# Retention and SwiGLU in one kernel: the output-weight sums of two quads per GpSimd instruction, the order of the second tile's first sums, and the place of tile 0's results

## The chip, the core and the metric

The kernel runs on one core of a Trainium2 chip. The metric is device time in microseconds (us), the median of several executions. A profile is one further execution, recorded by the hardware profiler; its span runs from the first to the last recorded instruction. The engines are named as in the profile: PE (matmul), DVE (vector), ACT (scalar), POOL (GpSimd) and SP, which here only issues transfers. "ACTq" and "SPq" are the transfers that ACT and SP issue.

## The reference

Retention for 8 batches and 8 heads, then a SwiGLU block over the 4608 tokens that come out of it. All of it is float32.

```
scores = scale * q @ k.T                       # per batch and head, 576 x 576, head size 64
ret = scores * D                               # D[i, j] = gamma_h ** (i - j) for i >= j, else 0
attn = ret @ v
x = attn.transpose(0, 2, 1, 3).reshape(4608, 512)
g, val = x @ w_gate, x @ w_val                 # 512 x 1536 each
out = (g / (1 + exp(-g)) * val) @ w_out        # 1536 x 512
```

## The kernel before

**Tiles.** The tokens are cut into tile 0 (512 tokens) and tiles 1 to 4 (1024 tokens each). A "tick" (`tick`) does the retention of one pair of heads: PE forms scores, states and values in the tiles `inner` and `outer`, and ACT, DVE and SP prepare the operands of the next pair. A pair needs its transposed keys (`kT`, L492), its scaled keys (`kn`, L507) and the masked scores (`ret`, L580). Ticks 10 to 13 stand between the down products of tile 0.

**Tile 0** is computed plainly: `up0` makes the twelve blocks `hid0[0]` to `hid0[11]` of the hidden activation, and `down0` (L864) multiplies them with the output weights in the order of `down_order`, four matmuls of 512 columns for each block, into the banks A, B, C and E. `out0` (L869, L870) then copies the four banks with ACT to `part[4:8]` and stores them.

**Tiles 1 to 4** use a fast matrix multiplication after Strassen and Winograd on two levels. The weights lie in three "quads" (`qd` 0 to 2). The up product of a quad goes through seven sets of operands, `SETS = (1, 2, 6, 7, 4, 5, 3)`. Outer sums make sets 5, 6, 7, 4 of the weights (`w_outer`) and 5, 6, 3, 7 of the tokens (`x_outer`); inner sums (`w_inner`, `x_inner`) make four further blocks of a set. A set in `PLAIN` goes without inner sums. In tile 1 and quad 0 these are sets 1, 4, 5 and 3, so that only sets 2, 6 and 7 need inner sums there. One step of the up product, called a slot here, is two matmuls (L1183) into one bank; a plain set has 8 slots, another has 7. The result of a slot is added from the bank by DVE (L1040) or copied by ACT (L1215); finished blocks go through silu on ACT (L1197) and a product on DVE or POOL (L1198) into `hid`.

**Sums of the weights.** In tile 1 POOL makes the sums of the up weights as it goes, and SP stores each set to memory (`store`, L1116 to L1119) for tiles 2 to 4, which load them. The sums of the output weights are made once, while tile 0 is computed (`out_sums`, L886): a list of events, `OUT_SUMS`, is gone through for each quad, and each of its 26 operands is stored with one transfer (L954, `dn<-rest`). POOL does quads 0 and 1, DVE quad 2. Two of the operands are needed negated for POOL, which ACT does (`negate`, L916). POOL's results go to 256-column places in `rest`, six at first and ten later; DVE's go to 22 places. A place is used again when its store has landed. The lists are emitted in groups of three operands, one group of DVE and one of POOL after each block of `down0`; POOL's first ten groups stand earlier, after blocks 10 and 11 of `up0`.

**Order.** All engines run a recorded program in order. The order of each engine's instructions, SP's transfers included, is the order in which the Python code issues them. At the end of tile 0 (`m >= 9`) `early_sums` puts the first sums of tile 1 behind POOL's sums of the output weights: `w_outer(5)`, `w_inner(1)` and its store, `w_outer(7)`, `w_inner(2)` and its store. The rest of quad 0's sums stand at slots of tile 1 in `up_stage` (`later(at, ...)`): x sums of set 2 at 0, of 6 at 10, of 7 at 18, of 1 at 28; weights of 6 (outer at 4, inner at 6), 7 (inner at 14), 4 (outer at 22, inner at 24), 5 at 32 and 3 at 37; set 1 of the next quad at 42. The two retention pairs that follow are loaded by SP behind slots 13 and 30.

**Places.** `part` lies in `rest` from `dn_at` on. `w_dn` of quad 0 is `part[0:4]`, and of quad 1 `part[4:8]`, so that these parts can be written only when POOL has read the output weights there and SP has stored those of them that are operands themselves. `hid` of quad 0 lies over `hid0[0]` to `hid0[7]`. Sets 6, 5 and 4 of the quad-0 weights are written over `hid0[1]` and `[3]`, `[4]` and `[6]`, `[5]` and `[7]`; each must wait until `down0` has read these.

Of the kernel before, what the change touches and what calls it, by code (L numbers as in the profile page):

```python
# [131 lines left out]
def kernel(  # L132
# [32 lines left out]
    nc = tc.nc  # L165
# [691 lines left out]
            nc.vector.tensor_tensor(out=hid0[f], in0=pair[1], in1=s, op=ALU.mult)  # L857


    down_order = [8, 9, 10, 4, 5, 11, 6, 7, 0, 1, 2, 3]  # L860

    def down0(f):
        for i, bank in enumerate(banks):
# [1 line left out]
                             start=(f == down_order[0]), stop=(f == down_order[-1]))  # L865

    def out0():
        for i, (bank, o) in enumerate(zip(banks, part[4:8], strict=True)):
            nc.scalar.copy(out=o, in_=bank)  # L869
            nc.sync.dma_start(out=out[i * P : (i + 1) * P, :], in_=o)  # L870

# [18 lines left out]

    pool_places = [rest[:, sum_at + TB * i : sum_at + TB * (i + 1)] for i in range(6)]
    more_places = [rest[:, raw_at + TB * i : raw_at + TB * (i + 1)] for i in range(16) if i % 4]
    x0_places = [rest[:, x0_at + TB * i : x0_at + TB * (i + 1)] for i in range(8)]
    vector_places = x0_places + more_places[6:] + [rest[:, part_at + TB * i : part_at + TB * (i + 1)] for i in range(8)]

    def events_of(text):
        r = []
# [12 lines left out]
    negatives = [x_odd[:, r, 640 : 640 + TB] for r in (2, 3)] + more_places[4:6]  # L912

    def negate(qd):
        for n, s in enumerate((3, 5)):
            nc.scalar.mul(out=negatives[2 * qd + n], in_=w_dn[:, qd, s // 2, s % 2], mul=-1.0)  # L916

    def out_sums(qd):
# [8 lines left out]
        eng, sum_places = (nc.vector, vector_places) if qd + 1 == NQ else (nc.gpsimd, pool_places)  # L927
        events = events_of(OUT_SUMS if qd + 1 == NQ else signed)

        def view(s):  # L930
            if s > 13:
                return negatives[2 * qd + s - 14]
            return w_dn[:, qd, s // 2, s % 2] if s < 8 else place[s]

        def used(e):
            return [e[1]] if e[0] is None else [int(a) for a in e[1][2:]]

        def release(k):

            for s in list(place):  # L940
                for e in events[k + 1 :]:
                    if s in used(e):
                        break
                    if s == e[0]:
                        free(place.pop(s))
                        break
                else:
                    free(place.pop(s))

        def do(k):  # L950
            e = events[k]
            if e[0] is None:
                _, slot, i = e
                nc.sync.dma_start(out=dn_ops[i][:, qd * TB : (qd + 1) * TB], in_=view(slot))  # L954
            else:
                new = sum_places.pop(0)
                add(eng, e[1], view, new)
                if e[0] in place:
                    free(place[e[0]])
                place[e[0]] = new  # L960
            release(k)

        r, ends = [], [k for k, e in enumerate(events) if e[0] is None]
        for g in range(0, N, 3):
            lo, hi = ends[g - 1] + 1 if g else 0, ends[min(g + 2, N - 1)] + 1

            def group(lo=lo, hi=hi):
                for k in range(lo, hi):
                    do(k)

            r.append(group)
        return r
# [121 lines left out]
    def w_sets(qd):  # L1094

        up = lambda n, k: w_up[:, qd, :, 2 * n : 2 * n + 2, k, :]
        sets = {1: up(0, 0), 2: up(0, 1), 7: up(1, 0), 3: up(1, 1), 5: hid[:, qd, 2:4, 0:2], 6: hid[:, qd, 0:2, 2:4], 4: hid[:, qd, 2:4, 2:4]}
        blocks = (extra_at(0, 1024), extra_at(1536, 1024), rest[:, x0_at + 1024 : x0_at + 2048])
        new = {o: blocks[(qd + i) % 3].rearrange("p (g j x) -> p g j x", g=2, j=4) for i, o in enumerate(SETS)}
# [12 lines left out]

        def store(o, new_ones):
            dst = up_sets[qd][SETS.index(o)]
            if new_ones:
                return [lambda: nc.sync.dma_start(out=dst[:, 6 * P :], in_=new[o].rearrange("p g j x -> p (g j x)"))]  # L1116
            raw = dst[:, 0 : 6 * P].rearrange("p (g x) -> p g x", g=2)
            return [lambda: nc.sync.dma_start(out=raw[:, :, P:], in_=sets[o][:, :, 0]),
                    lambda: nc.sync.dma_start(out=raw[:, :, 0:P], in_=sets[o][:, :, 1, P:])]  # L1119

        return sets, new, outer_sums, inner_sums, store

    def early_sums():

        x_outer = x_sets(1)[0]
        _, _, w_outer, w_inner, store = w_sets(0)
        p = [w_outer(5), w_inner(1) + store(1, True), w_outer(7), w_inner(2) + store(2, True)]
        v = [f for o in (5, 6, 3, 7) for f in x_outer(o, nc.vector)]
        return p, v

    def up_stage(n):
# [18 lines left out]
        def later(at, *fs):  # L1150
            after.setdefault(at, []).extend(fs)
# [288 lines left out]
        if t + AHEAD < NP:  # L1440
            load(t + AHEAD)

    groups = [(qd, group) for qd in range(NQ - 1) for group in out_sums(qd)]
    last_groups = out_sums(NQ - 1)
    todo = [m for m in range(3, len(order))]
    plan = []

# [8 lines left out]
    for f in range(2, NF):  # L1456
        round_until({4: 12, 6: 13, 8: 14, 9: 15, 10: 16, 11: 17}.get(f, f + 2))
        plan.append(lambda f=f: up0(f, range(HP)))
        if f - 1 in tick_at and f < 7:
            plan.append(lambda t=tick_at[f - 1]: next_load(t))  # L1460
        if f in tick_at and f > 2:
            plan.append(lambda t=tick_at[f]: tick(t, HP, FIRST))
            if tick_at[f] == HP + 1:
                plan.append(end_transposes)
        if f in (7, 10, 11):
            plan.append(lambda t=tick_at[f]: next_load(t))
        for _ in range({10: 7, 11: 3}.get(f, 0)):
            if f >= (7, 10, NF)[groups[0][0]]:
                if f + 1 == NF and more_places:
                    plan.append(lambda places=more_places[:4]: pool_places.extend(places))  # L1470
                    more_places.clear()
                if len(groups) % 9 == 0:
                    plan.append(lambda qd=groups[0][0]: negate(qd))
                plan.append(lambda group=groups.pop(0)[1]: group())
    assert not todo and len(groups) < 9
    for f in plan:
        f()
    tick_at = {1: 10, 3: 11, 6: 12, 8: 13}
    for m, f in enumerate(down_order):
# [5 lines left out]
        if last_groups:  # L1485
            last_groups.pop(0)()
        if groups:
            groups.pop(0)[1]()
# [12 lines left out]
    out0()  # L1501
    done = FIRST
# [59 lines left out]
```

## Time and profile before

| what | value |
| --- | --- |
| median of 3 runs | 1025.83 us (1025.13 to 1030.31) |
| the profiled execution | 1026.62 us, of which the span is 1024.9 us |
| DVE busy | 713.3 us (70%) |
| ACT busy | 286.3 us (28%) |
| POOL busy | 557.5 us (54%) |
| granted TensorE clock | full in all 40 slices |
| transfers | 194.38 MB, mean 190 GB/s |

Tile 0's up and down products end at about 176 us, tile 1's up product runs from there to about 329 us with ticks in its second half, and the down product of tile 1 follows. In the timeline view each line gives the start, the length, the engine, the line of the code, the operands and how many instructions were merged into it; in brackets stands how long the engine had been idle before it and what ended this. "x8" matmuls of L1183 are two slots, "x4" is one.

### The profile page before, as it was taken

How to read it: one execution, taken by the hardware profiler on the slowest of the kernel's cores; microseconds unless marked ns; L12 is line 12 of the kernel's file. 1: busy time of each engine (PE TensorE's matmuls, PEld its weight loads, DVE VectorE, ACT ScalarE, POOL GpSimd, SP SyncE). 2: the span in 40 equal slices, each digit the busy share in tenths (PEclk: the TensorE clock that was granted, in tenths of full speed). 3: DMA queues.
4: the chain of work that ended last, by engine and by line, in shares of the span. 5: the costliest groups of instructions: out<-in, count | busy, mean ns of one | idle time of the engine just before them, and what ended most of it. 6: DMA issues, size and time to landing. Idle time of an engine off the chain costs nothing.

```text
span 1024.9 us, 21387 instructions
## 1 busy us (share of the span) xinstructions
PE 1003.7 (98%) x8336; PEld 823.0 (80%) x8336; DVE 713.3 (70%) x1215; ACT 286.3 (28%) x638; POOL 557.5 (54%) x602
## 2 busy tenths in 40 slices
PE   6999989899999999999999999999999999999998
PEld 5654545788888888888888888888888888888887
DVE  5488877588787766876778688848585767566644
ACT  4465531122332411132332111133320012232110
POOL 3400178997563208665656247755582486566515
PEclk9999999999999999999999999999999999999999
DMA  9999877966496897656658767444455454445552
GB/s 244 253 272 239 202 203 247 275 202 176 120 266 157 221 238 225 194 157 174 187 181 225 195 186 210 148 141 144 157 193 155 144 185 154 143 147 188 175 161 100
DMA packets 281612, 194.38 MB, mean 190 GB/s; under 512 B 212968, under 2 KB 251112, under 8 KB 281512
## 3 DMA queue, kind: packets, MB, share of 16 engines
q1 hardware_dynamic: 247112, 93.52, 35.6%
q10 hardware_dynamic: 33760, 99.10, 29.5%
q8 instruction: 66, 1.08, 0.4%
q0 software_dynamic: 640, 0.39, 0.2%
q14 instruction: 34, 0.28, 0.1%
HBM read 154.04 MB, written 38.93 MB: 188 GB/s over the span
## 4 chain that ended last, share of the span: by engine, by line
PE 69%; DVE 2%; issue 1%; SPq 0%; DMA 0%; DVEq 0%; ACT 0%
PE bankC L1183 9%; PE bankB L1183 9%; PE bankA L1183 9%; PE bankE L1183 9%; PE bankB L1378 7%; PE bankE L1378 7%; PE bankC L1378 7%; PE bankA L1378 6%; PE outer L1183 2%; PE inner L1183 2%; DVE rest L1040 2%; PE outer L532 1%; PE outer L559 1%; PE inner L573 1%; PE inner L543 1%
## 5 line engine op out<-in xcount | busy, mean ns | idle before, releaser
L1040 POOL TENSOR_TENSOR rest<-rest 128x512 f32<-128x512 f32 (+1 forms) x141 | 150.3, 1077 | 156.1 <-DVE rest L1040 114.1
L1198 POOL TENSOR_TENSOR arena<-rest,io 128x256 f32<-128x256 f32 x156 | 113.8, 740 | 88.6 <-ACT io L1197 83.2
L1197 ACT ACTIVATE io<-rest 128x256 f32<-128x256 f32 x192 | 79.4, 417 | 212.0 <-DVE rest L1040 149.6
L1183 PE MATMUL bankB<-rest,arena 128*128 128x256 f32 x448 | 114.9, 381 | 1.0 <-DVE rest L1040 0.9
L1040 DVE TENSOR_TENSOR rest<-bankB,rest 128x512 f32<-128x512 f32 x116 | 78.5, 685 | 47.7 <-PE bankB L1183 32.2
L1183 PE MATMUL bankA<-rest,arena 128*128 128x256 f32 x412 | 105.4, 381 | 1.4 <-POOL rest L1040 0.9
L1183 PE MATMUL bankC<-rest,arena 128*128 128x256 f32 x416 | 106.4, 380 | 0.4 <-DVE rest L1040 0.2
L1040 DVE TENSOR_TENSOR rest<-bankA,rest 128x512 f32<-128x512 f32 x110 | 74.5, 684 | 45.9 <-PE bankA L1183 21.3
L1040 DVE TENSOR_TENSOR rest<-bankC,rest 128x512 f32<-128x512 f32 x110 | 74.7, 685 | 32.0 <-PE bankC L1183 18.9
L1183 PEld LDWEIGHTS bankB<-rest,arena 128*128 128x128 f32 x448 | 84.5, 190 | 13.8 <-POOL rest L1040 1.2
L1183 PE MATMUL bankE<-rest,arena 128*128 128x256 f32 x372 | 95.0, 380 | 0.4 <-DVE rest L1040 0.3
L1040 DVE TENSOR_TENSOR rest<-bankE,rest 128x512 f32<-128x512 f32 x106 | 71.8, 685 | 31.3 <-PE bankE L1183 14.8
L1183 PEld LDWEIGHTS bankA<-rest,arena 128*128 128x128 f32 x412 | 77.7, 190 | 13.6 <-DVE rest L1040 1.8
L1183 PEld LDWEIGHTS bankC<-rest,arena 128*128 128x128 f32 x416 | 78.3, 190 | 12.6 <-DVE rest L1040 1.4
L1040 POOL TENSOR_TENSOR arena<-arena 128x256 f32<-128x256 f32 (+1 forms) x80 | 74.4, 953 | 12.1 <-DMA up<-arena 6.2
L1183 PEld LDWEIGHTS bankE<-rest,arena 128*128 128x128 f32 x372 | 69.9, 190 | 11.7 <-DVE rest L1040 1.6
L886 POOL TENSOR_TENSOR rest<-rest 128x256 f32<-128x256 f32 x43 | 33.4, 800 | 53.8 <-DVE rest L407 36.6
L1378 PE MATMUL bankB<-arena 128*128 128x256 f32 x264 | 61.0, 381 | 0.0
L1378 PE MATMUL bankE<-arena 128*128 128x256 f32 x264 | 60.8, 380 | 0.0
L1378 PEld LDWEIGHTS bankE<-arena 128*128 128x128 f32 x264 | 49.9, 190 | 6.9
L1378 PEld LDWEIGHTS bankB<-arena 128*128 128x128 f32 x264 | 49.8, 190 | 6.9
L886 POOL TENSOR_TENSOR arena<-arena 128x768 f32<-128x768 f32 x24 | 47.0, 1961 | 15.3 <-DVE arena L1198 14.7
(267 smaller groups left out, 1881.1 us busy)
## 6 DMA issues: line engine op xcount, KB each, us to landing
arena<-up ACTq DMA_DIRECT2D x63, 896.0 KB, 4.6
arena<-dn ACTq DMA_DIRECT2D x65, 384.0 KB, 3.5
arena<-dn SPq DMA_DIRECT2D x39, 384.0 KB, 3.2
dn<-rest SPq DMA_DIRECT2D x78, 128.0 KB, 2.0
out_dram<-rest SPq DMA_DIRECT2D x35, 256.0 KB, 3.1
qk<-in_q_dram SPq DMA_DIRECT2D x108, 72.0 KB, 3.1
qk<-in_k_dram SPq DMA_DIRECT2D x108, 72.0 KB, 3.1
up<-arena SPq DMA_DIRECT2D x14, 512.0 KB, 2.9
```

The costliest lines, as they stand in the source:

```text
L532: m = nc.tensor.matmul(value(i, hl, c), s["v"][rows, at], ret[rows, c % 2 if whole(i) else hl, c // 2], start=start, stop=start, skip_grou ...
L543: nc.tensor.matmul(z[half[hl], r, c], s["kn"][chunk(i, hl, 2 * c + r)], s["v"][rows, at], start=True, stop=True, skip_group_check=True)
L559: nc.tensor.matmul(xr[half[hl]] if c + 1 == NC else value(i, hl, c), state[half[hl], c, :], s["qT"][half[hl], ts(c, L)], start=False, stop ...
L573: nc.tensor.matmul(sc[chunk(i, hl, 2 * c + r)[0], r if whole(i) else hl, c], kT[half[hl], at], qT[half[hl], at], start=True, stop=True, sk ...
L886: eng.tensor_tensor(out=dst, in0=srcs[0], in1=srcs[1], op=ALU.add if op[0] == "add" else ALU.subtract)
L1040: eng.tensor_tensor(out=out, in0=a, in1=b, op=ALU.add if sign > 0 else ALU.subtract)
L1183: m = nc.tensor.matmul(b[:, g * TB : (g + 1) * TB], w[:, g], x, start=(opens and g == 0), stop=True, skip_group_check=True)
L1197: nc.scalar.activation(out=s, in_=src[:, 0:TB], func=AF.Silu)
L1198: (nc.vector if busy and o != 2 else nc.gpsimd).tensor_tensor(out=hid[:, qd, 2 * H + h, 2 * T + t], in0=src[:, TB : 2 * TB], in1=s, op=ALU ...
L1378: nc.tensor.matmul(b[:, m * TB : (m + 1) * TB], lhs[:, qd, ts(m, P)], w[:, qd], start=(opens and qd == 0 and m == 0), stop=(qd == NQ - 1), ...
```

## The change

The sums of the output weights of quads 0 and 1 are made together: each POOL instruction of L886 works on 512 columns (256 of either quad) and each store of these carries both quads. POOL has seven places of 512 columns, all from the start; DVE's places go from 22 to 18. All nine groups of POOL now stand after blocks of `down0`, and both negations stand together behind `up0`, of 512 columns each. `down_order` reads the blocks that sets 6, 5 and 4 overwrite earlier and blocks 0 and 2 last; `out0` copies to these two and to `io`. The early sums are those of sets 2, 5 and 6, of weights and tokens. Set 1 of the weights of quad 0 is summed and stored at slot 28 of tile 1, and the blocks that hold inner sums take turns in another order in quad 0.

```
-    down_order = [8, 9, 10, 4, 5, 11, 6, 7, 0, 1, 2, 3]
+    down_order = [8, 9, 1, 3, 10, 4, 6, 11, 5, 7, 0, 2]
...
-        for i, (bank, o) in enumerate(zip(banks, part[4:8], strict=True)):
+        for i, (bank, o) in enumerate(zip(banks, (hid0[0], hid0[2], io[:, 0:512], io[:, 512:1024]), strict=True)):
             nc.scalar.copy(out=o, in_=bank)
             nc.sync.dma_start(out=out[i * P : (i + 1) * P, :], in_=o)
...
+    both = lambda lo, step: rest[:, lo : lo + 2 * step].rearrange("p (q x) -> p q x", q=2)[:, :, 0:TB]
+    pool_places = [both(sum_at + 2 * TB * i, TB) for i in range(3)]
+    wide_places = [both(raw_at + TB * i, TB * step) for i, step in ((1, 1), (3, 2), (9, 1), (13, 1))]
+    vector_places = x0_places + [rest[:, raw_at + TB * i : raw_at + TB * (i + 1)] for i in (11, 15)] + [rest[:, part_at + TB * i : part_at + TB * (i + 1)] for i in range(8)]
...
-    def negate(qd):
+    negatives = [x_odd[:, 2:4, 640 : 640 + TB], both(raw_at + 6 * TB, TB)]
+    def negate():
         for n, s in enumerate((3, 5)):
-            nc.scalar.mul(out=negatives[2 * qd + n], in_=w_dn[:, qd, s // 2, s % 2], mul=-1.0)
+            nc.scalar.mul(out=negatives[n], in_=w_dn[:, 0:2, s // 2, s % 2], mul=-1.0)
...
-                nc.sync.dma_start(out=dn_ops[i][:, qd * TB : (qd + 1) * TB], in_=view(slot))
+                nc.sync.dma_start(out=dn_ops[i].rearrange("p (q x) -> p q x", q=NQ)[:, qs], in_=view(slot))
...
+        turns = [(qd + i) % 3 for i in range(len(SETS))] if qd else (2, 1, 2, 0, 1, 0, 2)
+        new = {o: blocks[i].rearrange("p (g j x) -> p g j x", g=2, j=4) for i, o in zip(turns, SETS, strict=True)}
...
-        p = [w_outer(5), w_inner(1) + store(1, True), w_outer(7), w_inner(2) + store(2, True)]
+        p = [w_inner(2) + store(2, True), w_outer(5), x_inner(2, nc.gpsimd), w_outer(6), w_inner(6) + store(6, True), x_inner(6, nc.gpsimd)]
...
-            for o, at in {2: 0, 6: 10, 7: 18, 1: 28}.items():
+            for o, at in {7: 6, 1: 22}.items():
...
-                    outers, inners = {6: 4, 4: 22}, {6: 6, 7: 14, 4: 24, 5: 32, 3: 37}
+                    outers, inners = {7: 0, 4: 14}, {7: 2, 4: 18, 1: 28, 5: 35, 3: 39}
...
-                        later(at + 42 + j, f)
-                    later(at + 45, *next_store(1, True))
+                        later(at + (42 if qd else 44) + j, f)
+                    later(at + (45 if qd else 47), *next_store(1, True))
...
-        for _ in range({10: 7, 11: 3}.get(f, 0)):
...
+        if f + 1 == NF:
+            plan.append(lambda: pool_places.extend(wide_places))
+            plan.append(negate)
...
         if m >= 9:
+            for f in early_x[:4]:
+                f()
+            del early_x[:4]
             for f in [f for fs in early[:2] for f in fs]:
                 f()
             del early[:2]
-        if m >= 10:
-            for f in early_x[:4]:
-                f()
-            del early_x[:4]
```

More of the change, by code (lines that the diff above doesn't have):

```diff
@@ L889 @@
     dn_ops = [dr.tile([P, 768], F32, name=f"dn{i}") for i in range(N)]
-    pool_places = [rest[:, sum_at + TB * i : sum_at + TB * (i + 1)] for i in range(6)]
-    more_places = [rest[:, raw_at + TB * i : raw_at + TB * (i + 1)] for i in range(16) if i % 4]
     x0_places = [rest[:, x0_at + TB * i : x0_at + TB * (i + 1)] for i in range(8)]
-    vector_places = x0_places + more_places[6:] + [rest[:, part_at + TB * i : part_at + TB * (i + 1)] for i in range(8)]
+    both = lambda lo, step: rest[:, lo : lo + 2 * step].rearrange("p (q x) -> p q x", q=2)[:, :, 0:TB]
+    pool_places = [both(sum_at + 2 * TB * i, TB) for i in range(3)]
+    wide_places = [both(raw_at + TB * i, TB * step) for i, step in ((1, 1), (3, 2), (9, 1), (13, 1))]
+    vector_places = x0_places + [rest[:, raw_at + TB * i : raw_at + TB * (i + 1)] for i in (11, 15)] + [rest[:, part_at + TB * i : part_at + TB * (i + 1)] for i in range(8)]
     def events_of(text):
@@ L911, with out_sums @@
         signed[at[0]] = signed[at[0]].replace(old, new)
-    negatives = [x_odd[:, r, 640 : 640 + TB] for r in (2, 3)] + more_places[4:6]
-    def negate(qd):
+    negatives = [x_odd[:, 2:4, 640 : 640 + TB], both(raw_at + 6 * TB, TB)]
+    def negate():
         for n, s in enumerate((3, 5)):
-            nc.scalar.mul(out=negatives[2 * qd + n], in_=w_dn[:, qd, s // 2, s % 2], mul=-1.0)
-    def out_sums(qd):
+            nc.scalar.mul(out=negatives[n], in_=w_dn[:, 0:2, s // 2, s % 2], mul=-1.0)
+    def out_sums(last):
         place = {}
@@ L925, in free @@
                 sum_places.append(p)
-        eng, sum_places = (nc.vector, vector_places) if qd + 1 == NQ else (nc.gpsimd, pool_places)
-        events = events_of(OUT_SUMS if qd + 1 == NQ else signed)
+        qs = NQ - 1 if last else slice(0, NQ - 1)
+        eng, sum_places = (nc.vector, vector_places) if last else (nc.gpsimd, pool_places)
+        events = events_of(OUT_SUMS if last else signed)
         def view(s):
             if s > 13:
-                return negatives[2 * qd + s - 14]
-            return w_dn[:, qd, s // 2, s % 2] if s < 8 else place[s]
+                return negatives[s - 14]
+            return w_dn[:, qs, s // 2, s % 2] if s < 8 else place[s]
         def used(e):
@@ L1098, in w_sets @@
         blocks = (extra_at(0, 1024), extra_at(1536, 1024), rest[:, x0_at + 1024 : x0_at + 2048])
-        new = {o: blocks[(qd + i) % 3].rearrange("p (g j x) -> p g j x", g=2, j=4) for i, o in enumerate(SETS)}
+        turns = [(qd + i) % 3 for i in range(len(SETS))] if qd else (2, 1, 2, 0, 1, 0, 2)
+        new = {o: blocks[i].rearrange("p (g j x) -> p g j x", g=2, j=4) for i, o in zip(turns, SETS, strict=True)}
         def outer_sums(o):
@@ L1123, in early_sums @@
     def early_sums():
-        x_outer = x_sets(1)[0]
+        x_outer, x_inner, *_ = x_sets(1)
         _, _, w_outer, w_inner, store = w_sets(0)
-        p = [w_outer(5), w_inner(1) + store(1, True), w_outer(7), w_inner(2) + store(2, True)]
+        p = [w_inner(2) + store(2, True), w_outer(5), x_inner(2, nc.gpsimd), w_outer(6), w_inner(6) + store(6, True), x_inner(6, nc.gpsimd)]
         v = [f for o in (5, 6, 3, 7) for f in x_outer(o, nc.vector)]
@@ L1441, in next_load @@
             load(t + AHEAD)
-    groups = [(qd, group) for qd in range(NQ - 1) for group in out_sums(qd)]
-    last_groups = out_sums(NQ - 1)
+    groups, last_groups = out_sums(False), out_sums(True)
     todo = [m for m in range(3, len(order))]
@@ L1466 @@
             plan.append(lambda t=tick_at[f]: next_load(t))
-        for _ in range({10: 7, 11: 3}.get(f, 0)):
[L1468 to L1475, printed above, removed]
+        if f + 1 == NF:
+            plan.append(lambda: pool_places.extend(wide_places))
+            plan.append(negate)
+    assert not todo
     for f in plan:
@@ L1487 @@
         if groups:
-            groups.pop(0)[1]()
+            groups.pop(0)()
         if m == 9:
```

## Prediction

> **What bounds the kernel now.** I read the page first: PE is busy for 98% of the span and the chain of waits is 69% PE's, so an edit on another engine pays only where PE waits. The list of PE's waits names few of more than 0.2 us after the first 40 us, and PE's timeline places them:
>
> ```profile
> PE 1003.7 (98%) x8336; PEld 823.0 (80%) x8336; DVE 713.3 (70%) x1215; ACT 286.3 (28%) x638; POOL 557.5 (54%) x602
> PE 69%; DVE 2%; issue 1%; SPq 0%; DMA 0%; DVEq 0%; ACT 0%
> ...
> 139.33 0.46 PE L532 MATMUL outer<-ret,v 64*64 64x64 f32 x16 [0.95 <-ACT rest L626]
> 143.23 0.27 PE L567 MATMUL outer<-qT,kT 64*64 64x64 f32 x2 [1.55 <-DVE kT L492]
> 182.09 1.99 PE L1183 MATMUL bankE<-x_odd,arena 128*128 128x256 f32 x8 [0.93 <-ACT rest L869]
> 188.40 1.10 PE L1183 MATMUL bankB<-rest,arena 128*128 128x256 f32 x4 [0.86 <-DVE rest L1040]
> 198.13 1.13 PE L1183 MATMUL bankA<-rest,arena 128*128 128x256 f32 x4 [0.86 <-POOL rest L1040]
> 203.46 1.56 PE L1183 MATMUL bankC<-x_odd,arena 128*128 128x256 f32 x6 [0.31 <-POOL arena L1040]
> ```
>
> The first two waits stand in tick 11, the others in tile 1's first quad. The brackets understate them, since PE also restarts slowly, so I count by distances. Undisturbed, tick 12 starts 0.96 us after the pair of matmuls before it (153.50 to 154.46) and takes 2.26 (to 156.72), 3.22 in all. Tick 11 takes from 137.36 to 143.96, 6.60: it loses **3.38**. A slot takes 0.864 (190.20 to 195.38 are six). From 175.69 to 211.76 PE does 37 slots, 31.97 at that pace, in 36.07: it loses **4.10**. So at most 7.48 us can be had. (Another 1.06 of waits at 271 to 287 isn't touched.) What holds PE up is in the other engines' timelines:
>
> ```profile
> 133.91 0.39 ACTq L287 DMA_DIRECT2D kn<-in_k_dram  x1
> 135.40 0.39 ACTq L287 DMA_DIRECT2D v<-in_v_dram  x1
> 135.83 0.72 ACT L916 ACTIVATE rest<-rest 128x256 f32<-128x256 f32 x2 [11.63 <-DMA dn<-rest]
> 136.46 0.35 ACT L584 COPY even<-inner 128x256 f32<-128x256 f32 x1
> 181.45 0.59 ACT L869 COPY rest<-bankE 128x512 f32<-128x512 f32 x1 [3.58 <-DMA dn<-rest]
> ...
> 132.01 0.72 POOL L886 TENSOR_TENSOR rest<-rest 128x256 f32<-128x256 f32 x1 [12.05 <-DMA dn<-rest]
> 168.43 12.89 POOL L1040 TENSOR_TENSOR arena<-arena 128x512 f32<-128x512 f32 x12
> 197.35 0.73 POOL L1040 TENSOR_TENSOR rest<-x_odd 128x256 f32<-128x256 f32 x1
> 168.43 3.38 POOL L1040 TENSOR_TENSOR arena<-arena 128x512 f32<-128x512 f32 x2
> ...
> 168.94 3.42 DVE L1040 TENSOR_TENSOR rest<-x_odd,rest 128x512 f32<-128x512 f32 x2
> 140.01 1.82 DVE L886 TENSOR_TENSOR rest<-rest 128x256 f32<-128x256 f32 x2
> ```
>
> ACT issues a load (L282, L287) whose last transfers wait, one for one, for stores of sums that SP sends late; only then come the negations, and the copy L584 with which tick 11's chain begins. `out0` waits for stores out of `part`. POOL, with six places, stands still for 12 us; what PE misses at 198 and 203 comes last in its queue. The last three lines are for a cost below.
>
> **ACT and tick 11.** By the waits in the built program, kn's issue now waits for a piece issued at 125.76, and v's for SP's v load, issued at 126.60. SP's kn load, issued at 126.11, had landed when ACT went on at 130.35, after 4.2 us; v's, with 0.68 of issue, should land about 131.5, and ACT has issued v by 131.9. Two negations of 512 columns follow; at 0.59 each (the nearest row, ACT's 512-wide copy; the narrow ones took 0.36) L584 starts at 133.1 instead of 136.46. From there to the end of the transposed keys (143.18) it took 6.72: 139.8. PE wants them 1.57 into the tick (154.46 to 156.03), at 138.32 + 1.57 = 139.9. Just in time, but for this: the pair of negations at 115.88, which goes away, is worth nothing, as PE was fully busy there.
>
> **What wide sums cost DVE.** DVE's sum of 256 columns takes 0.42 with POOL idle (129.57) and 0.91 beside POOL's 0.73 (140.01, two in 1.82). At 168.94 both do 512 columns, and both slow to 1.7 an instruction; beside POOL's 256 DVE's 512 took 1.2 (172.28). So DVE waits 0.5 for each 256 columns of POOL, and a sum of DVE will wait 0.5 more. Two such sums stand in tick 11's chain (+0.75 if the first meets POOL half way: 140.6, 0.7 late), four before the next mask and three before tick 12's keys (+3.5: about 153.5, due at 153.3, 0.2 late), four or five before tick 13's mask, which had 0.69 to spare and then delays the copy of `outer` on ACT by about 0.5. Together 1.4, so 3.38 - 1.4: I take **2.0**. Bounds: 3.1 (no such wait) and 0 (the load lands 2 us later as well).
>
> [...]
>
> **POOL's sums.** 46 instructions of 256 columns (L886) become 23 of 512. When POOL stopped six were done; now one is, as the second needs a negation. From 133.1, 22 remain. Two 512-wide ones alone took 2.49 at 184.14, 1.25 each: 27.5, and 0.3 for each of 14 DVE sums beside them (before: 40 at 0.69, as four in 2.79 at 117.17, plus 4.2 is 31.8, and POOL took 36.5 with 4.4 of waits for stores). End: 164.8; before 168.47. There are seven places for up to six live sums, so almost every result waits for a store. A 256 KB store lands in 2.0 (the row of 128 KB) to 3.1 us (out_dram). The tightest is the eighth sum, due at 142.5: its store, behind DVE's second group on SP, leaves at about 139.0 and lands by 142.1. So SP, with 52 issues for 78, keeps up by half a microsecond; without this cover each sum would cost a store more. DVE's 18 places make it wait for stores of two groups earlier, landed some 5 us before.
>
> **POOL's order of need.** Inner 2 (4 x 0.73), outer 5 (2 x 1.27), x of 2, outer 6, inner 6, x of 6: 16.8, and 0.5 for each of DVE's eight x sums: 185.6, the first x of 6 at 183. Outer 7, inner 7 and the first x of 7: 191.7; the other three, one product and outer 4: 197. PE's slot s is due at 175.69 - 2.0 + 0.864 s: slot 15 (x of 6) 186.7, 20 (outer 7, ready 188) 191.0, 22 (x of 7) 192.7, 27 (outer 4) 197.0. Just enough at the last.
>
> **`out0`.** Copy A runs as before; B waits for the last down matmul, which still reads block 2; then C and E: done some 2 us behind that matmul, while bank B is used again after 1.75 and E after 5.3. The out stores now stand on SP behind those of sets 2 and 6, until about 183; silu needs `io` from slot 11, and a store lands in 3.1. DVE's adds no longer wait for out stores (188.40). All four waits of the quad should go, 4.10; the other bound is -0.1 (POOL at 1.44 a sum, its mean for 512 columns from 116 to 185: 4.2 late at slot 27). I take **3.8**.
>
> **What is late next.** Set 1's sums, four instructions and a 512 KB store, move to slot 28. The store falls behind ten loads that SP sends at slot 31 (before, 206.84 to 212.98; now to about 207). Inner 3 waits for its block until 210, so set 1 of the next quad is ready at 216; slot 54 is due at 220. Hidden, by 4 us. For the waits at 271 to 287 I count a loss of 0.3 from a changed phase.
>
> **Sum.** 2.0 + 3.8 - 0.3 = 5.5. The profiled execution took 1026.62 (1024.9 of it span) and comes to 1021.1; the median of the runs lies 0.79 lower: **1020.3**.
>
> **Rivals.**
> (a) Ticks fully repaired: the load lands a microsecond sooner, or DVE meets gaps of POOL. Against it: POOL has no gaps then. 3.1 + 3.8: 1018.9.
> (b) Tick 11 keeps all its loss: v lands late. The margin is nil, and transfers share 0.9 of the queues at that time. 3.8 - 0.3: 1022.3.
> (c) POOL is late again for slots 20 to 27. The margin at slot 27 is nil. At 1.37 a sum, 2.6 late: gain 2.9, 1022.9.
> (d) Slower: the two-quad operands, 2048 columns apart, cost POOL far more than contiguous ones. The place is POOL's queue from 133 to 197, the price 22 times the excess over 1.25. From 1.50 the 5.5 us are given back; at 2.21 a sum (the dearest POOL row, 128x768 from arena and rest) they end 21 later: 1041; at 1.75, 1031. Against it: 128x768 with three such pieces averages 1.96, no more a column than 512 at 1.27.
>
> **Chances.** Forecast 0.50, (a) 0.13, (b) 0.13, (c) 0.12, (d) 0.12. The range 1018.3 (all 7.48) to 1023.5 holds all but (d). About 0.5%, 5.1 us, is what a measurement tells from no change. Below 1020.7 lie (a) and three quarters of the forecast: 0.50. (b), (c) and the rest are within: 0.37. Slower is (d) and a bad (c): 0.13.
>
> **What would show it.** L584 of tick 11 at about 133, and a tick of 3.2 to 4.5 us; DVE's L886 at about 1.4; POOL's 23 of L886 ending near 165 with no wait of over 1 us for `dn<-rest` after 133; L869 in one go; slots 0 to 37 in 32.0 to 32.6 us. The forecast is wrong if L584 starts after 134.5, if POOL's sums end after 168, or if a new wait of over 1 us stands at slots 15 to 60.

## The result, and where the profile after shows it

The changed kernel took 1022.68 us (median of 17 runs, 1020.05 to 1027.34), the kernel before, run beside it, 1026.66 (17 runs): a ratio of 0.9961, with a 95% interval of 0.9948 to 0.9974. Two later series of the same kernel gave 1020.05 (6 runs; 0.9943, 0.9928 to 0.9958) and 1022.56 (9 runs; 0.9954, 0.9937 to 0.9972). So it gains 4 to 6 us; 5.5 were predicted. The profiled execution took 1024.83 us and its span is 1023.1, only 1.8 less than before. First the page of the changed kernel, its lines of busy time and of the chain of waits:

```profile
PE 1005.2 (98%) x8336; PEld 825.3 (81%) x8336; DVE 720.9 (70%) x1215; ACT 286.5 (28%) x636; POOL 555.2 (54%) x579
PE 90%; DVE 4%; DMA 3%; ACT 1%; issue 1%; SPq 1%; ACTq 0%; DVEq 0%
```

POOL has 23 instructions less and as much work; DVE has the same instructions and 7.6 us more. Lines of the code from 893 on have moved by one to three (L869 is the same, L916 is now L917, L954 L956, L1040 L1042, L1183 L1186, L1198 L1201). PE's timeline after, where it names a wait or takes up the down product again:

```profile
57.10 3.70 PE L853 MATMUL bankA<-rest,arena 128*128 128x512 f32 x8 [0.97 <-ACT io L856]
...
138.38 1.02 PE L864 MATMUL bankE<-rest,arena 128*128 128x512 f32 x2
139.33 0.46 PE L532 MATMUL outer<-ret,v 64*64 64x64 f32 x16
...
143.52 0.37 PE L567 MATMUL outer<-qT,kT 64*64 64x64 f32 x2 [2.45 <-DVE kT L492]
...
144.78 2.07 PE L864 MATMUL bankA<-rest,arena 128*128 128x512 f32 x2
146.65 1.09 PE L864 MATMUL bankB<-rest,arena 128*128 128x512 f32 x2
...
268.94 1.99 PE L1186 MATMUL bankC<-rest,arena 128*128 128x256 f32 x8 [0.24 <-DVE rest L1042]
281.05 1.13 PE L1186 MATMUL bankB<-x_odd,rest 128*128 128x256 f32 x4 [0.56 <-ACT rest L1231]
```

Between 144 and 268 us no wait is named: the four of tile 1's first quad are gone. The first wait of tick 11 is gone as well, but the second has grown from 1.55 to 2.45, and behind it a pair of down matmuls takes 1.87 instead of 0.96. Why, the table by stretches shows (busy us of each engine and number of instructions, then granted clock, share of DMA time and GB/s):

```profile
core 0: us, PE busy (x) PEld busy (x) DVE busy (x) ACT busy (x) POOL busy (x), PEclk, DMA share, GB/s
139.00:143.40 4.40, 2.07 (x101) 1.61 (x100) 4.40 (x6) 1.16 (x3) 4.40 (x5) 1.00 0.71 242
143.40:146.80 3.40, 3.28 (x39) 2.13 (x40) 3.37 (x5) 0.37 (x1) 2.44 (x3) 0.50 0.91 321
146.80:150.00 3.20, 3.20 (x9) 1.44 (x8) 3.06 (x10) 2.28 (x8) 3.20 (x3) 1.00 0.68 243
```

Behind the wait the granted clock was 0.50 for 3.4 us. The chain to the keys, from the timelines of ACT, DVE and POOL:

```profile
133.80 0.72 ACTq L287 DMA_DIRECT2D v<-in_v_dram  x1
134.57 0.63 ACT L917 ACTIVATE x_odd<-rest 128x512 f32<-128x512 f32 x1 [9.07 <-DMA rest<-in_k_dram]
135.11 0.61 ACT L917 ACTIVATE rest<-rest 128x512 f32<-128x512 f32 x1
135.63 0.35 ACT L584 COPY even<-inner 128x256 f32<-128x256 f32 x1
...
139.21 2.90 DVE L886 TENSOR_TENSOR rest<-rest 128x256 f32<-128x256 f32 x2
142.04 0.77 DVE L492 STREAM_TRANSPOSE qT<-qk 128x576 f32<-128x576 f32 x1
142.74 0.73 DVE L492 STREAM_TRANSPOSE kT<-qk 128x576 f32<-128x576 f32 x1
...
135.28 1.28 POOL L886 TENSOR_TENSOR rest<-x_odd,rest 128x512 f32<-128x512 f32 x1 [25.50 <-ACT x_odd L917]
...
163.14 5.49 POOL L886 TENSOR_TENSOR rest<-rest 128x512 f32<-128x512 f32 x4 [2.52 <-DMA dn<-rest]
168.60 7.38 POOL L1042 TENSOR_TENSOR arena<-arena 128x256 f32<-128x256 f32 x6
```

ACT still stands behind its load until 134.5. DVE's two sums ahead of the transposes take 1.45 each beside POOL's wide ones (before: 0.91). POOL ends its sums of the output weights at 168.6, no sooner than before.

All profiles hold the same 8336 matmuls, so the time between the same two matmuls can be compared. The second and third profile of the changed kernel are those of the runs e1_again and e9_changed below.

| stretch of PE's timeline, us | before | after | second | third |
| --- | --- | --- | --- | --- |
| start to the matmul at 56.15 (L853) | 56.15 | 57.10 | 56.07 | 57.00 |
| to the last pair of L864 before tick 11 | 81.21 | 81.28 | 81.21 | 81.23 |
| tick 11, to the next L864 | 6.60 | 6.40 | 3.66 | 5.02 |
| the eight matmuls of L864 from there | 3.54 | 4.51 | 3.54 | 3.54 |
| to slot 0 (ticks 12 and 13) | 28.20 | 28.20 | 28.20 | 28.20 |
| slots 0 to 37 | 36.07 | 31.94 | 31.94 | 31.94 |
| to the matmul at 335 us | 123.24 | 123.32 | 123.55 | 123.05 |
| to the last matmul | 685.72 | 685.75 | 685.60 | 686.24 |
| to the end of the span | 4.18 | 4.62 | 4.61 | 4.63 |

Read by rows: the first quad gains 4.13 us each time. Tick 11 with what follows it gives anything from a gain of 2.94 to a loss of 0.77. The first row differs between executions of one kernel by as much as between the kernels, so the 0.97 at 57 us can't be put down to the change.

### The profile page after: what moved, and what is told of

Its sections match the earlier page's. It is cut to its first block, busy times and chain, and to the rows that moved or that the text cites. A ratio compares the mean times of both kernels' runs of the same rounds, so it can differ in the third digit from the quotient of the medians.

```text
span 1023.1 us, 21315 instructions
## 1 busy us (share of the span) xinstructions
PE 1005.2 (98%) x8336; PEld 825.3 (81%) x8336; DVE 720.9 (70%) x1215; ACT 286.5 (28%) x636; POOL 555.2 (54%) x579
## 4 chain that ended last, share of the span: by engine, by line
PE 90%; DVE 4%; DMA 3%; ACT 1%; issue 1%; SPq 1%; ACTq 0%; DVEq 0%
PE bankC L1186 11%; PE bankB L1186 11%; PE bankA L1186 11%; PE bankE L1186 11%; PE bankB L1381 7%; PE bankE L1381 7%; PE bankC L1381 7%; PE bankA L1381 6%; PE bankA L853 2%; PE outer L532 2%; DVE rest L1042 2%; PE outer L1186 2%; PE inner L1186 2%; PE bankB L853 2%; PE bankC L853 1%; PE inner L573 1%
## 5 line engine op out<-in xcount | busy, mean ns | idle before, releaser
L1042 POOL TENSOR_TENSOR rest<-rest 128x512 f32<-128x512 f32 (+1 forms) x141 | 150.5, 1079 | 156.3 <-DVE rest L1042 114.2
L1201 POOL TENSOR_TENSOR arena<-rest,io 128x256 f32<-128x256 f32 x156 | 115.1, 749 | 81.5 <-ACT io L1200 81.0
L1186 PE MATMUL bankB<-rest,arena 128*128 128x256 f32 x448 | 114.8, 381 | 0.1
L1042 DVE TENSOR_TENSOR rest<-bankB,rest 128x512 f32<-128x512 f32 x116 | 78.4, 685 | 47.7 <-PE bankB L1186 33.1
L1186 PE MATMUL bankC<-rest,arena 128*128 128x256 f32 x416 | 106.4, 380 | 0.5 <-DVE rest L1042 0.2
L1186 PE MATMUL bankA<-rest,arena 128*128 128x256 f32 x412 | 105.3, 380 | 0.6 <-DVE rest L1042 0.4
L1042 DVE TENSOR_TENSOR rest<-bankA,rest 128x512 f32<-128x512 f32 x110 | 74.4, 684 | 38.8 <-PE bankA L1186 19.9
L1042 DVE TENSOR_TENSOR rest<-bankC,rest 128x512 f32<-128x512 f32 x110 | 74.7, 685 | 32.7 <-PE bankC L1186 20.5
L1186 PE MATMUL bankE<-rest,arena 128*128 128x256 f32 x372 | 95.0, 380 | 0.4 <-DVE rest L1042 0.3
L1186 PEld LDWEIGHTS bankB<-rest,arena 128*128 128x128 f32 x448 | 84.5, 190 | 12.7 <-DVE rest L1042 1.1
L1042 DVE TENSOR_TENSOR rest<-bankE,rest 128x512 f32<-128x512 f32 x106 | 71.8, 684 | 31.8 <-PE bankE L1186 15.2
L1186 PEld LDWEIGHTS bankC<-rest,arena 128*128 128x128 f32 x416 | 78.3, 190 | 12.7 <-DVE rest L1042 1.5
L1186 PEld LDWEIGHTS bankA<-rest,arena 128*128 128x128 f32 x412 | 77.9, 190 | 12.3 <-DVE rest L1042 1.8
L1186 PEld LDWEIGHTS bankE<-rest,arena 128*128 128x128 f32 x372 | 69.9, 190 | 11.8 <-DVE rest L1042 1.6
L1042 POOL TENSOR_TENSOR arena<-arena 128x256 f32<-128x256 f32 (+1 forms) x76 | 70.6, 952 | 9.1 <-DMA up<-arena 4.7
L886 POOL TENSOR_TENSOR rest<-rest 128x512 f32<-128x512 f32 x21 | 28.2, 1368 | 63.6 <-DVE rest L407 59.7
L886 POOL TENSOR_TENSOR arena<-arena 128x768 f32<-128x768 f32 x24 | 47.1, 1962 | 15.3 <-DVE arena L1201 14.6
```

What stands on the lines that cost most here:

```text
L886: eng.tensor_tensor(out=dst, in0=srcs[0], in1=srcs[1], op=ALU.add if op[0] == "add" else ALU.subtract)
L1042: eng.tensor_tensor(out=out, in0=a, in1=b, op=ALU.add if sign > 0 else ALU.subtract)
L1186: m = nc.tensor.matmul(b[:, g * TB : (g + 1) * TB], w[:, g], x, start=(opens and g == 0), stop=True, skip_group_check=True)
L1201: (nc.vector if busy and o != 2 else nc.gpsimd).tensor_tensor(out=hid[:, qd, 2 * H + h, 2 * T + t], in0=src[:, TB : 2 * TB], in1=s, op=ALU ...
```

## The experiments

**The changed kernel again (e1_again, e9_changed).** No edit.

> The changed kernel once more, unaltered. Theory N: what its first profile shows at 57.10 (0.97 us on a silu that follows a late weight load) and the lateness of the key chain of tick 11 come from when loads land, which differs from run to run; then the wait at 57 is gone or of another size here, L584 of tick 11 stands at another distance from the last pair of down matmuls before the tick (2.75 us ahead of it there), and the median stays within 1.5 us of 1022.7. Rival C: both come with the change; then the 0.97 stands again at the same place, to 0.2 us, and L584 at 2.5 to 3.0 ahead. In both, where PE waits over 2 us for L492 in tick 11 its clock is halved for about 3.4 us behind it, and where it waits under 1.5 it is not.

> The changed kernel unaltered, beside the next two on the same chip, to have their time against its own. Theory N: slots 0 to 37 take 31.9 to 32.0 us again, and everything else but the first 57 us and tick 11 agrees with its two earlier profiles to 0.5 us in the sum; tick 11 loses anything from 0.3 to 4.2 us. Median 1020 to 1023.

Medians 1020.05 and 1022.56. The wait at 57 us is absent in the second profile and stands again in the third (1.05). The one line of tick 11 that names a wait of over 0.2 us, and two lines of ACT's, in the second profile and then in the third:

```profile
140.21 0.27 PE L567 MATMUL outer<-qT,kT 64*64 64x64 f32 x2 [0.23 <-DVE kT L492]
...
130.12 0.39 ACTq L287 DMA_DIRECT2D kn<-in_k_dram  x1
132.33 0.35 ACT L584 COPY even<-inner 128x256 f32<-128x256 f32 x1
```

```profile
142.52 0.27 PE L567 MATMUL outer<-qT,kT 64*64 64x64 f32 x2 [1.60 <-DVE kT L492]
...
131.93 0.39 ACTq L287 DMA_DIRECT2D kn<-in_k_dram  x1
134.64 0.35 ACT L584 COPY even<-inner 128x256 f32<-128x256 f32 x1
```

In neither is the clock halved there (1.00 from 135 to 150 us). L584 started at 132.33 and 134.64, that is 4.95 and 3.59 us ahead of the last pair before the tick (137.28 and 138.23); in the first profile it was 2.75 (135.63 against 138.38). From L584 to the end of the keys it took 7.84, 7.82 and 7.83. PE wants the keys 0.96 + 1.57 = 2.53 behind that pair, so they are late by 7.83 - 2.53 = 5.30 less the lead: 2.55, 0.35 and 1.71, where the brackets, which understate a little, say 2.45, 0.23 and 1.60. Two later profiles with the same chain fit: with a lead of 4.53 (e8) the bracket says 0.66, with 5.52 (e3) there is no wait. One number of ACT's, the lead of L584, sets the tick.

The lead follows the loads. In the first profile ACT's v waited for SP's v load, issued at 128.58 and landed at 133.78. In the other two it was kn, the issue ahead of it, that waited, for a piece of ACT's own load (issued at 125.07 and 127.01, landed at 130.05 and 131.86), and v followed kn at once; SP's v load had been issued there 12.85 and 11.38 us ahead of the pair (at 124.43 and 126.85), in the first profile only 9.80. So theory N holds for tick 11. For the rest it is only half borne out: the first of the two medians lies 2.65 us below 1022.7, where 1.5 was allowed, and the wait at 57 us comes and goes with the execution. (It also stands in the profiles of e6 and e10 below, 2.67 and 1.69; whether the kernel before ever has it can't be told from its one profile.)

**One part alone (e2_order_only, e3_wide_only).** The first takes the new orders and the new places of the results, and keeps the sums of the output weights quad by quad; the second takes only the sums of two quads and the negations behind `up0`. The core of either:

```
-    down_order = [8, 9, 10, 4, 5, 11, 6, 7, 0, 1, 2, 3]
+    down_order = [8, 9, 1, 3, 10, 4, 6, 11, 5, 7, 0, 2]
...
-        p = [w_outer(5), w_inner(1) + store(1, True), w_outer(7), w_inner(2) + store(2, True)]
+        p = [w_inner(2) + store(2, True), w_outer(5), x_inner(2, nc.gpsimd), w_outer(6), w_inner(6) + store(6, True), x_inner(6, nc.gpsimd)]
```

```
+    pool_places = [both(sum_at + 2 * TB * i, TB) for i in range(3)]
...
+        qs = NQ - 1 if last else slice(0, NQ - 1)
...
+            plan.append(negate)
```

> The sums of the output weights quad by quad as before (40 and more of 256 columns on POOL, negations in two places), with the new order of the early sums, of the blocks of the down product and with the new places of the results. Theory O: the order alone earns the first quad, since POOL ended its sums of the output weights at 168.5 us in both kernels; slots 0 to 37 in 31.9 to 32.4 us without the four waits, tick 11 loses 3.4 as before; 1022.7, ratio to before 0.995 to 0.9975. Rival W: the wide sums with their 26 fewer stores make the room that the order needs; then SP's stores or POOL come late by 1 us and more at slots 15 to 27, and the ratio is 0.998 to 1.0.

> Before, with the sums of quads 0 and 1 in one operation and both negations behind the loads, and nothing else: the old order of the early sums and of the down product, results to the old places. Theory O: these earn nothing; the four waits of the first quad stay (3.5 to 4.5 us lost from slot 0 to 37), tick 11 loses 2.5 to 5 us as DVE's two sums ahead of the transposes take 2.9 instead of 1.8; ratio 0.999 to 1.0015. Rival W: the wide sums give about half of the gain: ratio 0.9965 to 0.9985, with the waits at 182 to 203 at half their size.

The order alone: 1023.74, ratio 0.9976 (0.9965 to 0.9987), between the two expectations. In its profile slots 0 to 37 take 32.64, tick 11 6.01, and from slot 37 to the matmul at 290 us it is 1.87 behind the kernel before (0.75 and 1.12). From its timelines of POOL and PE:

```profile
176.27 0.73 POOL L1040 TENSOR_TENSOR rest<-x_odd 128x256 f32<-128x256 f32 x1 [2.30 <-DMA dn<-rest]
...
199.00 1.56 PE L1184 MATMUL bankC<-x_odd,arena 128*128 128x256 f32 x6 [0.31 <-POOL arena L1040]
...
269.73 1.99 PE L1184 MATMUL bankE<-rest,arena 128*128 128x256 f32 x8 [0.48 <-DVE rest L1040]
272.20 1.13 PE L1184 MATMUL bankB<-x_odd,arena 128*128 128x256 f32 x4 [0.48 <-DVE rest L1040]
```

POOL's first token sum waits 2.3 us for a narrow store; from there POOL works without a stop up to what PE misses at 199.00, and the quad takes 0.70 more than in the changed kernel. The wide sums alone: 1025.99, ratio 0.9998 (0.9987 to 1.001), nothing. Slots 0 to 37 take 36.17, so the quad needs the order. Tick 11 took 3.21 in its profile, whole, but that was the fastest of its 12 runs (1024.72); how the tick went in the others isn't seen. Theory O is right on the wide sums by themselves and wrong that the order needs nothing else: the two ratios multiplied make 0.9974, and both together had 0.9943 on the same chip, 3.2 us more than the parts. (With the 0.9961 of the first series it is 1.3 us, which is within the noise.)

**DVE's sums out of the chain (e4_dve_first).**

```
-        if last_groups:
+        for _ in range((2, 0)[m] if m < 2 else min(1, len(last_groups))):
             last_groups.pop(0)()
```

> The changed kernel, with DVE's second group of sums (L879 and two L886) moved from behind the masks of tick 11 to where DVE stands idle, ahead of them (132 to 136 us); the order of SP's stores changes with it. Theory D: these two sums, 1.45 us each beside POOL's wide ones, are what makes the transposed keys late; they end 1.5 to 2.5 us sooner after L584 (5.3 to 6.3 instead of 7.77), the wait at L567 falls from 2.45 to under 0.8, the clock stays full, and the time is 1.5 to 2.5 under the unaltered changed kernel: about 1020.5. Rival A: ACT's late start is what counts, and DVE then only waits for the scaled queries (L489) in place of its sums: the keys end less than 0.7 sooner, the wait stays over 1.7, and the time within 0.7 of the changed kernel's.

The mechanism shows, the time does not. DVE's timeline, the two sums and the transposes:

```profile
131.07 0.75 DVE L886 TENSOR_TENSOR rest<-rest 128x256 f32<-128x256 f32 x2
137.24 0.69 DVE L580 TENSOR_TENSOR ret<-inner,near 128x512 f32<-128x512 f32 x1 [5.42 <-ACT even L584]
...
141.42 0.78 DVE L492 STREAM_TRANSPOSE qT<-qk 128x576 f32<-128x576 f32 x1 [1.37 <-ACT qk L489]
142.12 0.74 DVE L492 STREAM_TRANSPOSE kT<-qk 128x576 f32<-128x576 f32 x1
```

With POOL idle the two sums took 0.38 each, and the keys ended 6.00 behind L584 (136.86) instead of 7.84. L584 led the tick by 2.83, as little as in the first profile, and yet tick 11 took 3.95 with a full clock behind it (the second pair of down matmuls 0.96 behind the first), where that had 6.40 and 0.97 of slow matmuls. But the median was 1021.88 (ratio 0.9955, 0.9939 to 0.9971), and 1020.05 for the unaltered kernel on the same chip: no gain, where 1.5 to 2.5 was expected. Of what the tick gained in the profile, 0.34 ahead of slot 0 and 0.8 between 290 and 335 us came back; that executions with early loads have little to gain is argued, not seen.

**ACT's load behind tick 10 (e5_late_load, e6_late_dve).** The second has the edit of e4 as well.

```
-        if f in (7, 10, 11):
+        if f in (7, 10):
             plan.append(lambda t=tick_at[f]: next_load(t))
...
             go_on(2)
+            if m == 1:
+                next_load(9)
```

> The changed kernel, with ACT's load of the second pair after (L282, L287: ten transfers) issued behind the copies and scalings of tick 10 in place of ahead of the negations. Theory A: what ties tick 11 to the landing of earlier loads is that this issue stands ahead of the negations and of L584 in ACT's order; then L584 stands 4.5 us or more ahead of the last pair of down matmuls before tick 11, the tick loses under 0.6 of its 3.2 us pace, the clock is not halved there, POOL's sums begin at about 126 us and end 2 us and more sooner, and the median is 1019.3 to 1020.5, not over that of the unaltered changed kernel. Rival L: the transfers now land too late for the scalings of tick 12 (L507 and L489, some 10 us later), and that tick or the next loses 1 to 3 us in place of tick 11: 1021 to 1023.

> The same, and DVE's second group of sums ahead of the masks as in the run before. If theory A of that run holds, the keys of tick 11 are then early by 1 us and more and nothing is left to gain in the tick: the same to 0.7 us as without it. If DVE's sums beside POOL still set the keys there, it is 0.3 to 1.0 us faster.

1022.50 (ratio 0.9958, 0.9943 to 0.9974) and 1022.83 (0.9967, 0.9955 to 0.9978), the same to 0.7 us, as the second expectation had it. (The unaltered changed kernel was not run on this chip; its ratios on others were 0.9943 to 0.9961.) Tick 11 is whole (3.21 and 3.26), as theory A said, but the time is not what it forecast, and the rest goes as rival L said. From e5's timelines of ACT, PE and POOL:

```profile
140.01 5.71 ACTq L282 DMA_DIRECT2D rest<-in_k_dram  x4
...
147.53 0.37 ACT L584 COPY even<-inner 128x256 f32<-128x256 f32 x1 [11.44 <-DMA rest<-in_k_dram]
...
153.62 0.27 PE L567 MATMUL outer<-qT,kT 64*64 64x64 f32 x2 [0.83 <-DVE kT L492]
...
155.96 3.90 POOL L886 TENSOR_TENSOR rest<-rest 128x512 f32<-128x512 f32 x3 [5.11 <-DMA dn<-rest]
160.35 5.76 POOL L886 TENSOR_TENSOR rest<-rest 128x512 f32<-128x512 f32 x4 [0.49 <-DMA dn<-rest]
```

The same issue now stands ahead of tick 12's copy, and that tick takes 3.45 instead of 2.25. POOL starts 7 to 10 us sooner (its second sum at 124.91) and ends at 166.1 all the same: it waits 11.8 us for stores. PE comes to tile 1 earlier, POOL doesn't: POOL's sums end 7.2 us ahead of slot 0, in the changed kernel 8.8. Between slot 37 and 266 us 0.8 to 1.0 is lost; that this is the price of it is argued.

**The negations first (e7_neg_first).** The block with `plan.append(negate)` stands ahead of the one with `next_load`.

> The changed kernel, with the two negations ahead of ACT's load instead of behind it, and the load where it was. Theory A: L584 still waits for the load's last issue, and gains only the 1.1 us of the two negations; POOL begins 6 to 9 us sooner and ends its sums of the output weights at 157 to 163 us. Tick 11 loses 0 to 2.4, by how late the loads are in the profiled execution; median between that of the unaltered changed kernel and 1.0 less. Rival P: POOL's early start is what the ticks lack; then the tick is whole in any case, and the time that of the late load.

1022.88 (0.9965, 0.9946 to 0.9983): no gain over the ratios of the changed kernel. POOL began at 126.73 but ended at 167.4, not by 163: it waited 10.5 us for stores. L584 stood behind the load as before (at 137.58), and tick 11 took 5.29. Rival P falls.

**The results back to `part` (e8_out0_back).**

```
-        for i, (bank, o) in enumerate(zip(banks, (hid0[0], hid0[2], io[:, 0:512], io[:, 512:1024]), strict=True)):
+        for i, (bank, o) in enumerate(zip(banks, part[4:8], strict=True)):
```

> The changed kernel, with tile 0's results copied to part[4:8] again. Theory R: these places are still read by stores of sums when the copies want them, so L869 stalls on them (3.58 us before the change) and the waits of the first quad on bank E and on DVE's adds come back: 34.0 to 34.5 us for slots 0 to 37 instead of 31.94, 2.3 us slower than the unaltered changed kernel. Rival S: with wide stores and POOL done sooner the places are free in time: 31.9 to 32.4, the same time.

1028.81, slower than the kernel before (1.0017, 1.0004 to 1.0029): slots 0 to 37 take 37.87. From its timelines of SP and PE, and then two stretches with their granted clock (last but two):

```profile
185.24 0.32 SPq L1119 DMA_DIRECT2D up<-rest  x1
185.66 2.58 SPq L870 DMA_DIRECT2D out_dram<-rest  x4
...
189.51 1.64 PE L1186 MATMUL bankA<-rest,arena 128*128 128x256 f32 x4 [3.57 <-DVE rest L1042]
```

```profile
185.94:189.90 3.96, 0.39 (x3) 0.39 (x3) 0.69 (x1) 0.00 (x0) 3.92 (x5) 1.00 0.98 375
189.90:193.30 3.40, 2.89 (x8) 1.84 (x7) 1.89 (x3) 0.42 (x1) 3.24 (x5) 0.51 1.00 325
```

Theory R has the wait on DVE's adds right, but not where it comes from, nor its size: ACT's copies are done by 179.5. The out stores stand on SP behind the store of set 6, which waits for POOL until 185.2; DVE's adds (L1042) want `part` before that (the one at 188.68 had waited 8.79 us, until an out store landed), PE stands for 3.57, and its clock is halved for 3.4 us. So the new order would cost more than it brings without the dead places: they are worth 5.9 us here.

**Only kn and v behind tick 10 (e10_late_kv, e11_late_kv_neg).** The second has e7's edit too. In `load`:

```
+                    send = lambda dst=dst, src=src: queue.dma_start(...)
+                    if i == needed(1) - 3:
+                        put_off.append(send)
...
             go_on(2)
+            while put_off:
+                put_off.pop(0)()
```

> The changed kernel; of ACT's load only kn and v (L287, two transfers) are issued behind the copies and scalings of tick 10, the eight of q and k stay where they were. Theory A: the negations and L584 then wait for no landing of SP's v load; L584 stands 4.5 us or more ahead of the last pair before tick 11, which loses under 0.8, and tick 12 takes its 2.25 since q and k are there in time; median 0.5 to 2 under the unaltered changed kernel. Rival B: as with the whole load put off, what tick 11 gains is lost again by 240 us, since POOL's sums, held by their stores, end no sooner than 164 us while PE comes to them sooner: the time within 0.5.

> The same, and the negations ahead of the load. Theory A: L584 waits for PE or for the last issue of k only; tick 11 loses under 0.3 in any execution; POOL begins at about 126 us and waits for stores (as with the whole load put off, 11 us in all); median 0 to 0.7 under the kernel before it. Rival B: the same as for it: the gain of the tick comes back as waits at slots 15 to 60.

1021.48 (0.9950, 0.9938 to 0.9962) and 1020.93 (0.9946, 0.9935 to 0.9958), five runs each; the changed kernel on the same chip 1022.56. Tick 11 is whole in both profiles (3.21), tick 12 takes 2.34 and 2.25, and slots 0 to 37 31.94: theory A. The lines of e10 that count (its lines stand five further on, so L589 is L584 and L869 L864):

```profile
133.42 0.37 ACT L589 COPY even<-inner 128x256 f32<-128x256 f32 x1 [1.36 <-issue]
136.00 0.39 ACTq L287 DMA_DIRECT2D kn<-in_k_dram  x1
136.42 0.82 ACTq L287 DMA_DIRECT2D v<-in_v_dram  x1
...
139.33 1.02 PE L869 MATMUL bankE<-rest,arena 128*128 128x512 f32 x2
142.54 1.12 PE L869 MATMUL bankA<-rest,arena 128*128 128x512 f32 x2
```

The lead is 139.33 - 133.42 = 5.91, over the 5.30 that the tick needs. In e11 it is only 3.84, and the tick is whole because POOL waited for a store while DVE made its sums (0.41 each); the keys then ended 6.15 behind the copy instead of 7.83. In e7, with POOL as early, it was so too (6.02). By the medians they beat the changed kernel by 1.1 and 1.6 us, but the intervals of the ratios overlap: likely, not shown.

## Why the prediction was nearly right, step by step

- **First quad, 3.8.** Measured 4.13 in all three profiles, and all four waits gone, as the steps on POOL's order, on `out0` and on slot 54 had it. The margins "nil" at slot 27 held, although POOL ended its sums up to 3.8 us later than the 164.8 forecast: PE came later too. From POOL's end to slot 0 the forecast has 173.7 - 164.8 = 8.9 us, and 8.9, 8.8 and 8.8 were measured; in e5 and e6, with 7.2 and 6.2, the quad takes 32.11 and 32.65. So the distance was forecast rightly, while its two ends moved by 4.7 and 4.8 us between the executions. POOL's 22 sums took 33.3, 31.9 and 31.9 us where 31.7 were worked out. The forecast that no wait for `dn<-rest` would be over 1 us was wrong (2.52 in the first profile, 1.32 and 1.23 in the others); SP did not keep up by half a microsecond, and e7 shows that stores, not POOL, set that end.
- **Tick 11, 2.0.** This is the step that failed, as "Just in time": -0.77, 2.94 and 1.58 were measured. The first lies outside the bounds given, 0 to 3.1. A lead of 4.26 (137.36 - 133.1) was forecast and 2.75, 4.95 and 3.59 came. Of the two waits that the forecast names, the one it reckons by, v's for SP's v load, ended last in the first profile alone: that load was issued 0.96 later against the pair than forecast (9.80 ahead instead of 10.76) and landed 5.2 behind its issue instead of 4.9. In the other two it was kn's wait, for a piece of ACT's own load. A fixed time from one profile was put in the place of a spread, with no margin left. The chain behind L584 was 7.83 where 7.47 was worked out: DVE's two sums took 2.90 together, where 1.82 + 0.75 was counted, so neither found POOL half way. And the halved clock, 0.97 us on the down matmuls and 0.5 within the tick, was no term at all.
- **Dearer sums of DVE.** Forecast 1.41 each (0.91 and 0.5 more); the 20 of L886 have a median of 1.36, and none took over 1.50. But the 0.7 that these sums were to cost ticks 12 and 13 wasn't there: the stretch to slot 0 is 28.20 in both kernels.
- **Removed negations, nothing; later waits, -0.3.** Up to tick 11 PE keeps its 81.2; from slot 37 to 335 us it is -0.1, -0.3 and +0.2.
- **Not in the sum:** 0.44 more from the last matmul to the end of the span (with either part alone it is 4.18 and 4.26). The last stores are issued at the same distance; what takes longer behind them stays open.
- **Rivals.** (b), the tick keeps its loss, is the first profile; (a), fully repaired, nearly the second. Which of them an execution shows is decided by its loads, so they were not alternatives. That a median of the changed kernel, which mixes such executions, falls close to 1020.3 or 2.4 above it is in part luck. (c) came only with the narrow sums (0.31 at 199.00 in e2). (d) falls: POOL's two-quad sums took 1.27 without DVE beside them, no more than contiguous ones (1.27 in the rows of 512 columns before).
- **The signs named beforehand.** By two of its three signs the first profile speaks against the forecast: L584 starts at 135.63, after 134.5 (134.64 in the third), and POOL's sums end at 168.6, after 168. The third sign, a new wait of over 1 us at slots 15 to 60, is nowhere. The signs were times from the start of the span; what counted were distances, L584's to the pair and POOL's to slot 0.

## What to carry to other kernels

Where a chain starts behind an instruction that waits for a landing, its start is a spread and not a number (L584's lead came out at 2.75, 4.95 and 3.59 us): write down the lead that the consumer needs (here 5.30 us) and count the repair as a mean over the lead's range. Keep the issue of a transfer that nobody needs soon out of the way of work that somebody waits for, but look what that issue is ahead of in its new place: the whole load moved cost tick 12 what tick 11 gained, its last two transfers didn't. A reordering is worth what its places allow: the same order with the results in `part` was slower than no change (1028.81 against 1026.69).

## What the runs showed of the hardware that was not expected

A wait of 2.45 us cost PE 1.5 more through its clock: 0.97 on the eight matmuls behind the tick, and 0.5 within the tick, since 6.40 is 0.73 more than 3.22 and the wait, where 3.66 and 5.02, with a full clock, are 0.21 and 0.20 more. In the trace of the changed kernel the granted clock is 0.5 from 143.37 to 146.78, 3.41 us, and PE had worked for 1.1 of the 3.41 us before that (139.96 to 141.07). In e8 it had worked 0.4 (0.39 of the 3.96 us up to 189.90, and then 3.4 us at a clock of 0.51). In e6 a wait of 2.67, before a matmul at 58.87, left the clock full: the eight matmuls behind it took 3.70, as did those behind the 0.97 at 57.10. So the length of a wait alone doesn't decide it. The recorded changes of the clock stand whole steps of 3.4133 us apart: those at 17.08, 143.37, 146.78 and 1024.01 in the changed kernel's trace 37, 1 and 257 steps, those at 12.11 and 1025.87 in the trace of before 297. Counted in such steps from e6's next recorded change (1023.96), its wait falls into two of them, and PE worked 1.6 in the first. In the traces of the changed kernel and of the one before there are 592 such steps from the first recorded change to the last: PE worked 1.11 us in one and not at all in two (the last ones, behind its last matmul), and the clock was half behind these three; in all others it worked 1.69 us or more, and the clock was full behind them. So the same wait is dear or not by where it falls in these steps. How much work is enough, the traces don't say to the tenth: counted in this way in the others, the clock was half behind steps with 0.72 (e4, 20.98 to 24.40), 1.61 (e7, from 21.10), 1.65 (e3, from 15.06) and 1.73 us (e8, from 22.68), and full behind steps with 1.62 (e6), 1.72 (e10, from 55.99) and 1.82 us (the third profile, from 139.92). One halved step lowers the mean granted clock of a span by 0.0017; the means are 0.998 in e4, e7 and e3, 0.996 in e8 with its two, and 1.0, 0.999 and 1.0 in the last three. From 1.61 to 1.73 us both occur.
